# Six more of the late tiles' products joined into sevens of quarter products, and the left-hand sums of three joins moved to GpSimd

## Chip, cores and metric

One NeuronCore of a Trainium2 chip. The metric is the device time of one launch in microseconds (us). Before the change it is 378.43 us, the median of three runs (378.24 to 379.07).

## What is computed

Attention with softmax over 8 batches, 12 heads, 448 tokens and head width 64, followed by a feed-forward layer with a SiLU-gated hidden layer on the same 3584 tokens. Cut to what matters:

```python
scores = scale * np.matmul(q, k.transpose(0, 1, 3, 2))
attn = np.exp(scores - max); attn = attn / sum
x = np.matmul(attn, v)   # as (3584, 768)
h = x @ w_in             # (3584, 2048)
g = h * (1.0 / (1.0 + np.exp(-h)))
return g @ w_out         # (3584, 768), float32
```

The change touches the last product alone, g @ w_out, for the rows that are computed last.

## The kernel before, in words

The rows of the output are cut into 28 tiles of 128 tokens, and two neighbouring tiles make a **quad** (qd 0 to 13). For a quad, the product with w_out is a 2 by 2 block product: two row tiles against the two halves of the hidden dimension, and these against the two halves (384 columns each, `OH`) of w_out. The kernel does it with **seven block products instead of eight** (Winograd's form of Strassen's scheme). The products are numbered m = 1 to 7; each is eight matmuls (`HF` = 8 hidden tiles of 128) of 128x384. Their left operands are blocks of the hidden values `G` (and `X`, a copy of one tile of `G`) or sums of such blocks (`S`, written by DVE in `combine_g`, two instructions of 128x512 for each sum; product 7's sum is written over `G`). Their right operands are blocks of w_out or differences of them (`D4`, `D5`, `D6`). PSUM results are copied to `ost` tiles by ACT (`take_copy`, products 1, 5, 6, 4) or added to them by DVE (`take_sum`, products 2, 7, 3), and stored by DMAs from SP and ACT.

A **fold** goes one level deeper. The same product m of two quads a and b has the same right operand; so the two left operands, of two different quads, stand above each other and make another 2 by 2 block product, with the eight hidden tiles cut 4 and 4 and the 384 columns cut 192 and 192. A fold does it with seven products of four matmuls of 128x192 (`fold_product`, k = 1, 4, 6, 5, 7, 3, 2 in two PSUM banks `n_..._P` and `n_..._Q`) instead of 16 matmuls of 128x384. It needs four sums of left blocks (`fold_x`, 128x512 f16, by DVE, L1065) and, once for each m, four differences of right blocks (`fold_w`, 128x768, by DVE, L1047). `fold_read` adds the results into the output tiles (DVE, L1101 to L1113), or copies the first of them where the fold is listed in `AHEAD_OF` (ACT, L1097). Before, `FOLD` (L254) names three folds: m = 2 and m = 4 of quads 10 and 11, and m = 4 of quads 12 and 13.

**The order of all work is laid out ahead of time** by a planner in the kernel (`Order`, L111, `step`, L160): it keeps a clock for each engine, gives each operation a planned cost, and appends the instructions to the engines' queues in the order in which it thinks that they become ready. TensorE (PE) takes from the list `moe` the first entry whose inputs are ready in the planner's time. On the chip, every engine then goes through its queue strictly in that order and waits on semaphores. The costs in the planner are its author's numbers (0.40 for an instruction of `combine_g`, 0.43 for one of `fold_x`, for instance); they only set the order.

The end of the kernel is in this order: the hidden values of the last two pairs of batches (products `f`, L683 through `times`, read by ACT and DVE), then quads 10 to 13. GpSimd (POOL) issues the loads of q, k, v and the weights and has nothing to do after the last of them.

Rings limit how far engines may run ahead: `S` has three buffers (`NSG`), `ost` four (`NOST`); some quads' output tiles lie in old buffers instead (`FAR` in the `xT` ring, `WIDE` in two `E` slots).

Of the kernel before, what the change touches and what calls it, by code (L numbers as in the profile page):

```python
# [110 lines left out]
class Order:  # L111


    def __init__(self, shy):
        self.now, self.shy = 0.0, shy
        self.free = {"PE": 1.0, "ACT": 2.1, "DVE": 1.2, "POOL": 1.2}
        self.wait = {"ACT": [], "DVE": []}
        self.pool = []
        self.sent = []
        self.dma_free = 0.0  # L120
        self.out = []
        self.mode = None
        self.drawn, self.crossed = 0, [0.0]
        self.busy = {e: 0.0 for e in self.free}
# [35 lines left out]
    def step(self):  # L160

        soon = []
        for eng in ("ACT", "DVE"):
            if self.free[eng] > self.now:
                soon.append(self.free[eng])
                continue
            best, urgent = None, None
            for op in self.wait[eng]:
                at = op.ready()
                if at is None:  # L170
                    continue
                if at > self.now:
                    soon.append(at)
                    if op.bias <= -10 and (urgent is None or at < urgent):
                        urgent = at
                elif best is None or (rank(op), at + op.bias) < best[0]:
                    best = ((rank(op), at + op.bias), op)
            if best and best[1].bias >= 0 and eng == "DVE" and urgent is not None:
                if urgent < self.now + self.shy * best[1].busy:
                    continue  # L180
            if best:
                self.wait[eng].remove(best[1])
                self.start(best[1])
                soon.append(self.free[eng])
        if self.free["POOL"] > self.now:
            soon.append(self.free["POOL"])
        elif self.pool:
            op, took, ring, gate = self.pool[0]
            at = 0.0
            if ring is not None:  # L190
                at = ring.when(1)
            if at is not None and len(self.sent) >= LOADS:
                at = max(at, self.sent[-LOADS].done + HOP)
            if at is not None and gate is not None:
                g = gate()
                at = None if g is None else max(at, g)
            if at is not None and at <= self.now:
                self.pool.pop(0)
                if ring is not None:
                    ring.take()  # L200
                self.start(op)
                self.sent.append(op)
                took += DMA_SLOW if len(self.sent) == 3 else 0.0
                few = len(self.sent) < 7
                start = self.now + DMA_START + (0.0 if few else DMA_LATE)
                self.dma_free = max(self.dma_free, start) + took
                op.done = self.dma_free + DMA_TAIL + (0.0 if few else DMA_MORE)
                soon.append(self.free["POOL"])
            elif at is not None:
                soon.append(at)  # L210
        return soon
# [3 lines left out]
def kernel(  # L215
# [36 lines left out]
    FAR = (NT * B // 4 - 3, NT * B // 4 - 1)  # L252
    WIDE = (NT * B // 4 - 6, NT * B // 4 - 4)
    FOLD = ((10, 11, (2, 4)), (12, 13, (4,)))  # L254
    AHEAD_OF = ((1, 4),)
# [649 lines left out]
    def combine_g(qd, m, f0, f1):  # L905
        a, b = 2 * qd, 2 * qd + 1
        if m != 7 and (qd, m) not in S_t:
            S_t[(qd, m)] = sb.tile([128, HF, 128], FP16, name=f"S_{qd}_{m}", tag="S", bufs=NSG)
# [12 lines left out]

    def product(qd, m, f0, f1, strips, c0=0, c1=OH):
        w = {1: rows(2 * qd, 0), 2: rows(2 * qd, 1), 4: rows(2 * qd + 1, 1), 7: rows(2 * qd + 1, 0)}
        w = w[m] if m in w else S_t[(qd, m)]
        if BANK[m] == m and f0 == 0:
            pr_t[(qd, m)] = psum_bank(f"p_{qd}_{m}" + "r" * (c0 > 0))
        if c1 - c0 < OH:
            half_t[c0] = pr_t[(qd, m)]
        for f in range(f0, f1):
            times(  # L930
                pr_t[(qd, BANK[m])][:, 0 : c1 - c0],
                w[:, f, :],
                W_[m][:, f, c0:c1],
                f == 0 and BANK[m] == m,
                f == HF - 1,
                strips,
            )
# [24 lines left out]
    def ost(qd, i, j):  # L962
# [4 lines left out]
        elif qd in WIDE:  # L967
            at, x = int(i != j), j
            if (qd, at) not in wide_t:
                wide_t[(qd, at)] = sb.tile(  # L970
                    [128, HG, S], FP16, name=f"wide_{qd}_{at}",
                    tag=f"E{e_slot[f'sx_{PAIRS[0]}_{at + 1}']}", bufs=1,
# [42 lines left out]

    def take_last(qd):
# [12 lines left out]
    def left(q, m, k):  # L1029
        return rows(2 * q + m // 4, 1)[:, 4 * k : 4 * k + 4]  # L1030
# [3 lines left out]

    def right_sum(m, i):
        n = 4 * (m // 4) + i - 1
        t = w_in_t[:, n % NDC, DFF // 2 * (n // NDC) : DFF // 2 * (n // NDC) + 2 * OH]
        return t.rearrange("p (f n) -> p f n", f=4)
# [10 lines left out]
    def fold_x(g, m, i, at):  # L1049
# [3 lines left out]
        if tag == "KT":  # L1053
# [11 lines left out]
        nc.vector.tensor_tensor(out=x2_t[(g, m, i)], in0=x, in1=y, op=op)  # L1065

    def fold_product(g, m, k):
# [12 lines left out]
        if k in (1, 4):  # L1080
            t = ps.tile([128, 2, 512], FP32, name=f"n_{g}_{m}_{bank}", tag="s", bufs=2)
            n2_t[(g, m, bank)] = t[:, 0, :]
# [4 lines left out]
    def fold_read(g, m, k):  # L1087
        a, b = FOLD[g][:2]
        i, j = {2: SUM[2], 4: OUT[4]}[m]
# [163 lines left out]
    far_ring, wide_ring = Ring(NX3), Ring(0)  # L1253
# [170 lines left out]
    def queue_pair_f(pb, f):  # L1424
# [23 lines left out]
        def queue(m):  # L1448
# [6 lines left out]
            def run():  # L1455
# [8 lines left out]
                if pb == PAIRS[0] and f == (3 if FILL < 4 else HF - 1) and m == 4:  # L1464
                    last_pair.append(op)
                    for _ in range(4):
                        wide_ring.give(op.done)
                if m == 1:
# [17 lines left out]
            def deps():  # L1486
# [14 lines left out]
                if before is not None:  # L1501
                    made.append((before.get(m), 9.0))
                if m == 1:
# [80 lines left out]
    def plan_sums():  # L1584
# [12 lines left out]
        while todo and (todo[0] == 7 or sg_ring.can(1, od.now)):  # L1597
            m = todo.pop(0)
            if m != 7:
# [23 lines left out]
    def plan_folds():  # L1623

        last = PAIRS[1]
        if "w" not in w2_op and (last, 5) in pair_done:
            made = [pair_done[(last, f)].get(m) for f in range(6) for m in range(1, 8)]
            if None not in made:
                w2_op["w"] = True
                for m in sorted({m for *_, ms in FOLD for m in ms}):  # L1630
                    for i in (1, 2, 3, 4):
                        more = [w2_op[(m, i // 2)]] if i in (2, 4) else []
                        w2_op[(m, i)] = od.add(
                            Op("DVE", 0.57, lambda m=m, i=i: fold_w(m, i), made + more, 1)
                        )
        if not folds or (last, HF - 1) not in pair_done:
            return
        g, m, done = folds[0]
        made = [x for q in FOLD[g][:2] for f in range(HF, NFF) for x in gates_at(2 * q + m // 4, f)]
        made += [pair_done[(last, HF - 1)].get((i, j)) for i in range(2) for j in range(2)]  # L1640
        n = len(x2_op) // 4
        if n > 1:
            made += [fold_done[n - 2].get(k) for k in (7, 2)]
        if None in made:
            return
        folds.pop(0)
        homes = [("KT", 3)] * 3 + [("rk", NRK)] if n % 2 else [("rq", NRQ)] * 4
        for i in (1, 2, 3, 4):
            more = [x2_op[(g, m, i // 2)]] if i in (2, 4) else []
            x2_op[(g, m, i)] = od.add(  # L1650
                Op("DVE", 0.43, lambda i=i: fold_x(g, m, i, homes[i - 1]), made + more, 1)
# [5 lines left out]
    def queue_fold(g, m):  # L1657
# [4 lines left out]
        first = {2: 1, 4: 4}[m]  # L1662
        early = (g, m) in AHEAD_OF
        if early:
            ahead[a] = lambda: when([reads.get(2)])
            ahead[b] = lambda: when([reads.get(7)])
        home = {q: far_ring if q in FAR else wide_ring if q in WIDE else ost_ring for q in (a, b)}

# [5 lines left out]
        def queue(k):  # L1674
            rings = ((s_ring, 1),) if k in (1, 4) else ()
# [3 lines left out]
            def run():  # L1679
                op = Op("PE", 4 * mm(OH // 2), lambda: fold_product(g, m, k), tail=PE_OUT)  # L1680
                for ring, need in rings:
                    ring.take(need)
                od.on_pe(op, "full", 4)
                done[k] = op
                narrow, wide = OH / 1920.0 + 0.13, OH / 960.0 + 0.13
# [6 lines left out]
                elif k == 7:  # L1692

                    def then(at):
                        s_ring.give(at)
# [8 lines left out]
                elif k == 2:  # L1704

                    def then(at):
                        s_ring.give(at)
# [5 lines left out]
            def deps():  # L1713
                made = [done.get(x) for x in {6: (1,), 5: (4,), 7: (6, 5), 3: (5,), 2: (3,)}.get(k, ())]
                made += [reads.get(x) for x in {6: (1,), 7: (6,), 3: (5,)}.get(k, ())]
                if not early:
                    made += [took_of[a].get(first)] if k == 1 else [took_of[b].get(first)] if k == 4 else []
                if (g, m) == TAIL and k in (2, 3):
# [8 lines left out]
                if not i:  # L1727
# [4 lines left out]
            moe.append((deps, 0, run, rings))  # L1732
# [6 lines left out]
    def queue_quad(qd):  # L1739
        quads.append((qd, [5, 6, 7, 3]))  # L1740
        took = {}
        home = far_ring if qd in FAR else wide_ring if qd in WIDE else ost_ring
# [13 lines left out]
        def queue(m, f0, f1, c0=0, c1=OH):  # L1756
            first = {6: (1,), 2: (1,), 7: (6, 5), 3: (5, 6) if qd == LAST else (5, 6, 7), 4: (7,)}.get(m, ())

            def run():
# [7 lines left out]
                if BANK[m] == m and f0 == 0:  # L1767
                    take_bank(f"p_{qd}_{m}" + "r" * (c0 > 0))
# [14 lines left out]
                read(m, [op] + [took[x] for x in {2: (1,), 7: (5,), 3: (6,)}.get(m, ())])  # L1783
                if m == 7 and (qd, 4) in folded:
                    if qd in ahead:
                        def then(at):
# [8 lines left out]
                                [op, took[7], ahead[qd]],  # L1795
# [7 lines left out]
            def deps():  # L1803
# [4 lines left out]
                made += [took.get(x) if x in hard else (took.get(x), 9.0) for x in first]  # L1808
# [8 lines left out]

            rings = ((home, 1),) if f0 == 0 and (m in OUT or m == 7 and (qd, 4) in folded and qd not in ahead) else ()
            moe.append((deps, int(BANK[m] == m and f0 == 0), run, rings))


# [6 lines left out]
        for m in (1, 5, 6, 2, 7, 3, 4) if qd < LAST else (1, 5, 6, 7, 3, 4):  # L1828
            if m == (3 if TAIL and qd == LAST else 4):
                for g, (a, b, ms) in enumerate(FOLD):  # L1830
                    for k in ms if max(a, b) == qd else ():
                        if (g, k) not in AHEAD_OF:
                            queue_fold(g, k)
# [449 lines left out]
```

## Time and profile before

| | us |
|---|---|
| median of three runs | 378.43 |
| the profiled execution | 378.51 |
| its span, first to last instruction | 376.7 |
| PE busy | 370.6 |
| DVE busy | 284.5 |
| ACT busy | 255.6 |
| POOL busy | 85.0 |

The span lies 1.8 us inside the profiled execution's time. "Busy" counts the time in which at least one instruction of the engine runs; a PE that is always busy may still be waiting for the next matmul's turn in its pipeline, and the time from one matmul's start to the next says more than the length of one. A group line gives line, engine, operation, output and inputs, count, busy us and mean ns. A window line gives for each engine its busy us and, in brackets, its instructions.

### The profile page before, as it was taken

The page shows a single profiled execution, that of the slowest core. Times are in us where ns is not written, and L with a number is a line of the kernel's source. Part 1 is how long each engine was busy: PE and PEld are TensorE (multiplying, and loading weights), DVE is VectorE, ACT ScalarE, POOL GpSimd, SP SyncE. Part 2 cuts the span into 40 slices and gives each one's busy share as a digit, 9 for nine tenths or more (in the row PEclk, how much of TensorE's full clock was granted, in tenths as well). Part 3 has the DMA queues.
Part 4 walks back from the last instruction along what each step waited for, and adds up shares of the span by engine and source line. Part 5 has one row for each costly group of instructions (what it writes and reads, how often), then busy time and mean ns, then how long its engine had stood idle before and what let it go on. Part 6 is the DMA issues. An engine that isn't in the chain of part 4 may idle for free.

```text
span 376.7 us, 9950 instructions
## 1 busy us (share of the span) xinstructions
PE 370.6 (98%) x4018; PEld 187.2 (50%) x4018; DVE 284.5 (76%) x588; ACT 255.6 (68%) x401; POOL 85.0 (23%) x155
## 2 busy tenths in 40 slices
PE   7999999999999999999999999999999999999996
PEld 3365445444444444444444454545556655556764
DVE  3668859899995969995969998899375425489953
ACT  4988873896878787877788777658872238883130
POOL 6652438324016326006423200000000000000000
PEclk9999999999999999999999999999999999999999
DMA  7999999919049848147955411210002330001334
GB/s 121 185 208 210 206 204 198 189 19 132 17 96 153 153 50 124 27 99 107 170 91 72 55 44 44 54 33 0 0 3 56 88 92 19 0 0 29 83 104 125
DMA packets 35967, 34.47 MB, mean 91 GB/s; under 512 B 11857, under 2 KB 35153, under 8 KB 35921
## 3 DMA queue, kind: packets, MB, share of 16 engines
q0 software_dynamic: 25312, 22.82, 40.8%
q1 hardware_dynamic: 10064, 10.38, 10.2%
q8 instruction: 31, 0.51, 0.6%
q10 hardware_dynamic: 544, 0.64, 0.5%
q14 instruction: 16, 0.12, 0.1%
HBM read 45.61 MB, written 11.01 MB: 150 GB/s over the span
## 4 chain that ended last, share of the span: by engine, by line
PE 95%; DVE 1%; ACT 1%; DMA 1%; issue 0%; DVEq 0%; POOLq 0%
PE p L683 30%; PE h L683 21%; PE f L683 16%; PE s L446 11%; PE a L568 8%; PE o L683 3%; PE a L554 2%; PE a L601 2%; PE n_Q L683 1%; DMA rk<-in_k_dram 1%; ACT T L491 1%; PE n_P L683 1%; PE z L683 0%; PE z L2185 0%; PE z L554 0%
## 5 line engine op out<-in xcount | busy, mean ns | idle before, releaser
L502 ACT ACTIVATE E<-s 128x896 f16<-128x896 f32 x164 | 141.9, 923 | 24.5 <-PE s L446 24.5
L683 PE MATMUL h<-xT,w_in_t 128*32 128x448 f16 (+2 forms) x762 | 83.5, 348 | 0.0
L683 PEld LDWEIGHTS <-w_in_t 128*128 128x128 f16 (+1 forms) x909 | 54.6, 97 | 50.0 <-issue 8.1
L352 POOL DMA_DIRECT2D V<-in_v_dram x88 | 48.5, 560 | 50.7 <-PE a L568 29.3
L683 PEld LDWEIGHTS <-G 128*128 128x128 f16 (+1 forms) x672 | 42.4, 97 | 29.5 <-issue 5.0
L715 ACT ACTIVATE th<-h 128x448 f16<-128x448 f32 x67 | 36.6, 546 | 24.2 <-PE h L683 21.0
L683 PE MATMUL p<-w_out_t,G 128*128 128x384 f16 (+2 forms) x326 | 50.6, 324 | 0.0
L446 PE MATMUL s<-rq,KT 32*128 32x448 f16 (+3 forms) x728 | 45.0, 347 | 1.5 <-DVE rq L410 1.0
L683 PEld LDWEIGHTS <-S 128*128 128x128 f16 (+1 forms) x321 | 29.5, 98 | 22.3 <-issue 3.4
L1004 ACT COPY ost<-p 128x384 f32<-128x384 f32 x42 | 20.1, 479 | 29.2 <-PE p L683 22.8
L759 DVE SCALAR_TENSOR_TENSOR G<-th,h 128x448 f16<-128x448 f16 (+1 forms) x64 | 35.6, 572 | 4.7 <-ACT th L715 4.3
L683 PE MATMUL p<-D,S 128*128 128x384 f16 (+1 forms) x217 | 38.8, 326 | 0.0
L1023 DVE TENSOR_TENSOR ost<-p,ost 128x384 f32<-128x384 f32 x31 | 17.1, 552 | 22.2 <-ACT ost L1004 14.5
L568 PE MATMUL a<-E,V 128*32 128x448 f16 (+1 forms) x640 | 32.7, 356 | 0.0
L332 POOL DMA_DIRECT2D rq<-in_q_dram x25 | 14.0, 559 | 68.1 <-PE s L446 59.0
L671 DVE SCALAR_TENSOR_TENSOR xT<-a,rdn 128x448 f16<-128x448 f32 x46 | 26.9, 618 | 2.9 <-PE a L568 2.2
L446 PEld LDWEIGHTS <-KT 32*128 32x128 f16 (+1 forms) x824 | 12.4, 96 | 31.7 <-issue 29.5
L515 DVE TENSOR_TENSOR T<-T,E 128x1792 f16<-128x1792 f16 x21 | 22.8, 1085 | 4.8 <-ACT E L502 4.8
L515 DVE TENSOR_TENSOR T<-E,E 128x1792 f16<-128x1792 f16 x21 | 22.7, 1082 | 4.0 <-ACT E L502 4.0
L886 DVE TENSOR_TENSOR p<-f,p 128x448 f32<-128x448 f32 x15 | 9.3, 623 | 19.2 <-PE f L683 11.5
L683 PE MATMUL f<-sx,tw 128*128 128x448 f16 x102 | 23.4, 352 | 0.0
L568 PEld LDWEIGHTS <-V 128*32 128x32 f16 (+1 forms) x640 | 13.5, 95 | 18.1 <-issue 10.1
(128 smaller groups left out, 455.1 us busy)
## 6 DMA issues: line engine op xcount, KB each, us to landing
out_dram<-ost SPq DMA_DIRECT2D x163, 48.0 KB, 1.7
rk<-in_k_dram POOLq DMA_DIRECT2D x24, 224.0 KB, 5.2
rq<-in_q_dram POOLq DMA_DIRECT2D x23, 224.0 KB, 5.8
w_out_t<-in_moe_w_out_dram POOLq DMA_DIRECT2D x4, 768.0 KB, 12.9
V<-in_v_dram POOLq DMA_DIRECT2D x42, 64.0 KB, 4.3
V<-in_v_dram POOLq DMA_DIRECT2D x42, 48.0 KB, 4.6
w_in_t<-in_moe_w_in_dram POOLq DMA_DIRECT2D x6, 256.0 KB, 8.7
w_in_t<-in_moe_w_in_dram POOLq DMA_DIRECT2D x3, 512.0 KB, 12.5
```

What stands on the lines that cost most here:

```text
L332: nc.gpsimd.dma_start(out=rawq[n][:, cols], in_=group_of(q, b, hg)[:, cols])
L352: nc.gpsimd.dma_start(out=VT[b][32 * x : 32 * (x + 1), hs, at : at + count, :], in_=v[b, hs].rearrange("h (i g) d -> i h g d", g=TPP)[:, : ...
L446: nc.tensor.matmul(out=pS[p0 : p0 + 32 * (x1 - x0), h % 2, at : at + q1 - q0], lhsT=KT[(b, hg)][32 * h : 32 * (h + 1), key_rows(b, hg, c, ...
L502: nc.scalar.activation(out=E[(n, w)][:, 2 * y : 2 * y + 2, :], in_=pS_t[(n, w, y)][:, :, 0:S], func=AF.Exp, scale=attn_scale,)
L515: nc.vector.tensor_tensor(out=T[n], in0=T[n] if step else E[(n, 0)], in1=E[(n, step + 1)], op=ALU.add,)
L568: nc.tensor.matmul(out=a[32 * h : 32 * (h + 1), 0:S], lhsT=VT[b][k0:k1, HG * hg + h, place(b, hg, c), part - 1 :: 2], rhs=e[k0:k1, h], sta ...
L671: nc.vector.scalar_tensor_tensor(out=x3(b, cc)[:, cc % 3, 32 * g0 : 32 * g1], in0=acc[(n, part)][:, 0:nq], scalar=0.5, in1=rdn_t[n].rearra ...
L683: nc.tensor.matmul(out=out[i : i + cut], lhsT=w[:, i : i + cut], rhs=x, start=start, stop=stop, skip_group_check=True,)
L715: nc.scalar.activation(out=th, in_=h_t[(b, f, t0)][:, 0:n], func=AF.Tanh)
L759: nc.vector.scalar_tensor_tensor(out=dst[:, f, at + lo : at + hi], in0=th_t[(b, f, t0)][:, lo - t0 : hi - t0], scalar=1.0, in1=h_t[(b, f, ...
L1004: nc.scalar.copy(out=ost(qd, *OUT[m]), in_=bank(qd, BANK[m]))
L1023: nc.vector.tensor_tensor(out=t, in0=bank(qd, BANK[m]), in1=t, op=ALU.add)
```

## The change

- `FOLD` now names six folds: also m = 5 of quads 10 and 11, m = 5 of quads 12 and 13, and m = 4 of quads 7 and 8. Six products of the quads (5 of 10, 11, 12, 13; 4 of 7 and 8) thus go from eight matmuls of 128x384 each to their share of seven times four of 128x192.
- The left operands of the folds with m = 5 are the sums `S_..._5`, which now lie in four old buffers of their own. Product 5's result belongs to two output tiles; a new DVE instruction, `take_mix`, adds the one output tile to the other (f32, 128x384, both in SBUF), once for each of quads 10 to 13.
- The four `fold_x` sums of the three folds (0, 2), (0, 4) and (1, 4), that is of m = 2 and m = 4 of quads 10 and 11 and m = 4 of quads 12 and 13, are written **by GpSimd** instead of DVE: 12 instructions of 128x512 f16 with two SBUF inputs. The build puts an instruction that reloads GpSimd's library ahead of the first.
- The differences of right operands for m = 2 and m = 4 are made earlier (beside quads 7 to 9) and into other buffers; four new ones for m = 5 take their place beside the last pair.
- Quad 11's output tiles lie in `E` slots (`BROAD`) instead of `xT` tiles; the fold of quads 7 and 8 uses PSUM banks of the ring `m` instead of `s`; the order in which the planner lays out the last 100 us is another one.

```diff
-    FAR = (NT * B // 4 - 3, NT * B // 4 - 1)
+    FAR = (NT * B // 4 - 1,)
+    BROAD = NT * B // 4 - 3
-    FOLD = ((10, 11, (2, 4)), (12, 13, (4,)))
-    AHEAD_OF = ((1, 4),)
+    FOLD = ((10, 11, (5, 2, 4)), (12, 13, (5, 4)), (7, 8, (4,)))
+    MID = 2
+    AHEAD_OF = ((0, 5), (1, 5), (1, 4))
...
+    def take_mix(qd):
+        t = ost_t[(qd, *OUT[6])]
+        nc.vector.tensor_tensor(out=t, in0=t, in1=ost_t[(qd, *OUT[5])], op=ALU.add)
...
     def left(q, m, k):
-        return rows(2 * q + m // 4, 1)[:, 4 * k : 4 * k + 4]
+        x = S_t[(q, 5)] if m == 5 else rows(2 * q + m // 4, 1)
+        return x[:, 4 * k : 4 * k + 4]
...
-        nc.vector.tensor_tensor(out=x2_t[(g, m, i)], in0=x, in1=y, op=op)
+        eng = nc.gpsimd if (g, m) in ((0,2),(0,4),(1,4)) else nc.vector
+        eng.tensor_tensor(out=x2_t[(g, m, i)], in0=x, in1=y, op=op)
...
             x2_op[(g, m, i)] = od.add(
-                Op("DVE", 0.43, lambda i=i: fold_x(g, m, i, homes[i - 1]), made + more, 1)
+                Op(
+                    *(("POOL", 1.3) if (g, m) in ((0,2),(0,4),(1,4)) else ("DVE", 0.43)),
+                    lambda i=i: fold_x(g, m, i, homes[i - 1]),
+                    made + more,
+                    1,
+                )
             )
```

## Prediction

> **What bounds the kernel now.** I read the page first: busy time, the slices, the chain that ended last. Then the last 40 us in windows, the timeline there, and the groups of DVE and POOL.
>
> ```profile
> PE 370.6 (98%) x4018; PEld 187.2 (50%) x4018; DVE 284.5 (76%) x588; ACT 255.6 (68%) x401; POOL 85.0 (23%) x155
> ...
> POOL 6652438324016326006423200000000000000000
> PEclk9999999999999999999999999999999999999999
> ...
> PE 95%; DVE 1%; ACT 1%; DMA 1%; issue 0%; DVEq 0%; POOLq 0%
> ```
>
> PE holds 95% of the chain at full clock; what shortens PE's list shortens the run, unless PE must wait. POOL is idle from the 24th slice (about 226 us) on. The windows of the last stretch (us, busy of PE, PEld, DVE, ACT, POOL):
>
> ```profile
> 330.00:340.00 10.00, 10.00 (x58) 5.50 (x57) 8.53 (x18) 7.82 (x17) 0.00 (x0) 1.00 0.00 0
> 340.00:350.00 10.00, 10.00 (x70) 6.41 (x68) 10.00 (x30) 2.87 (x6) 0.00 (x0) 1.00 0.16 42
> 350.00:360.00 10.00, 10.00 (x93) 7.99 (x92) 7.93 (x21) 2.55 (x6) 0.00 (x0) 1.00 0.30 75
> 360.00:370.00 10.00, 10.00 (x67) 6.28 (x66) 5.46 (x13) 1.91 (x4) 0.00 (x0) 1.00 0.33 95
> ```
>
> PE has no gap here, and DVE is full from 340 to 350: 10.00 of 10.00. In that window DVE writes the sums that PE multiplies next, so this is the second bound. ACT and the DMAs have room.
>
> **PE's part.** The timeline of PE (start, length; a row's length reaches past the next row's start because matmuls overlap):
>
> ```profile
> 343.12 1.46 PE L683 MATMUL p<-w_out_t,G 128*128 128x384 f16 x8
> 344.42 0.65 PE L683 MATMUL p<-D,S 128*128 128x384 f16 x3
> ...
> 348.49 0.49 PE L683 MATMUL n_P<-w_in_t,fold 128*128 128x192 f16 x4
> 348.82 0.49 PE L683 MATMUL n_Q<-w_in_t,fold 128*128 128x192 f16 x4
> ```
>
> Eight matmuls of 128x384 take 344.42 - 343.12 = 1.30 us, four of 128x192 take 0.33. A fold replaces two products, 2.60 us, by seven fours, 2.31 us. It saves 0.29; three more folds save **0.87 us**.
>
> What PE newly waits for: in the order after the change, the last hidden-layer product is followed by eight matmuls of p_11_1 (1.30), one four of n_0_5_P (0.33), and then n_0_5_Q, which needs both halves of S_10_5 and S_11_5 at once; before, only S_10_5 was needed so early. The four DVE instructions can begin when ACT's last writes of G allow, about 338.5 to 338.65 (the first was at 338.49), follow each other by 0.33, and the last takes 0.42: 340.1, as PE arrives. I allow 0.1 us there and 0.1 for two or three small waits later: 0.2. Without other effects the execution goes from 378.51 to 378.51 - 0.87 + 0.2 = **377.84**.
>
> **What lies beside other work.** DVE, from 338 on: four fewer fold_x (-4 x 0.33; twelve go to GpSimd, eight for m = 5 come), four take_mix and four more fold_read of about 0.55 each (no row has take_mix; the nearest, ost<-n_Q,ost of the same shape, takes 550 ns), or 0.47 when they follow each other: -1.3 + 3.8 = +2.5 us. DVE is idle for 2.07 us in 350 to 360 and 4.54 in 360 to 370, where the take_mix stand, so it costs nothing if the sums keep their places; uncovered, it costs up to 2.5. The eight fold_w of m = 2 and 4 (0.55 each) and four fold_x for quads 7 and 8 move to 280 to 295, where DVE is busy 4.59 of 6 (282 to 288) and 2.79 of 6 (288 to 294): nothing. ACT swaps four copies for six fold reads, of 10 us a window it uses 2.9: nothing. The stores keep their number (203 on SP); some of quads 7, 10 and 11 change places in SP's queue, and with a DMA share of 0.16 to 0.33 they hold up nobody. The end (last product, take_end, its store) is as it was.
>
> **GpSimd's sums.** No row shows GpSimd adding tiles. Its MEMSET of 64x256 takes 330 ns, one of 128x1 about 106: 0.88 ns for an element, 0.45 us for a pass over 512. From below: as fast as DVE's fold_x, 0.41. From above: two reads and a write one after the other, 0.11 + 3 x 0.45 = 1.45. I take two passes, 1.0 us. Their place has room: the first four need only G, can start at 338.5, and PE reads the first of them (fold_0_2_2, third in GpSimd's queue) after 47 matmuls of 384 and eight or nine fours, about 10.5 us after 339.8. The tightest is fold_1_4_2, third of the last four: inputs free at 357, read at 364. Each may take 2.3 us before PE waits. The library reload stands behind GpSimd's last load with no wait, 110 us before its first use: nothing.
>
> [...]
>
> **The step that decides: DVE and GpSimd side by side.** All 12 GpSimd sums read two SBUF tiles, in three bursts of four; beside them DVE runs sums with two SBUF inputs. In the order after, DVE has 26 of these in a row from 338.65. No row shows both engines reading. The nearest:
>
> ```profile
> L916 DVE TENSOR_TENSOR S<-G x26: 404/417/427, 93.3 to 358.5; 128x512 f16<-128x512 f16 x26
> ```
>
> From 93 to 226 us GpSimd issued loads beside these sums, later it did nothing, and minimum and maximum differ by 23 ns: issuing loads does not hurt DVE. But that is not reading tiles. So the ends are: no effect, 0; and taking turns, each DVE sum waiting for a GpSimd sum to finish. DVE has nothing to give in the first burst: 26 x 25 ns = 0.65 us, a lengthening by 6%, already eats the gain. Behind a DVE sum that is held stand all later sums and the reads that free PE's banks. I therefore take **turns**, with this price. Burst one: the four DVE sums that PE waits for stand behind four GpSimd sums, 4 x 1.0, less 0.3 for what PE has in hand: 3.7. Burst two (fold_0_4, about 346 to 351): DVE's run of two-input sums ends soon, then come reads from PSUM; one GpSimd sum counts: 0.8. Burst three (357 to 362): beside S_13_3 and the fold_1_5 sums, which PE needs within 3 us: half of 4, less some slack: 1.5. Together 6.0: 377.84 + 6.0 = **383.8 us**. With 0.55 for a sum (one pass, 0.11 + 0.45) it is 3.3 and 381.1; with 1.45, 8.7 and 386.5. If DVE's run goes first and GpSimd waits for its end at 347.5, the first fold sums come at 350.5 or later and the later ones push on: about half, 381. The case's own range is 380 to 386.8.
>
> [...]
>
> **The rivals.**
>
> 1. *Side by side without harm* (faster or no change). Place: the DVE sums beside a GpSimd sum. Price: none, so 377.84, between 377.6 (all waits gone, 378.51 - 0.87) and 378.2. For it: the row of S<-G. Against: these are loads. It decides as soon as a DVE sum beside a GpSimd sum is lengthened by less than 25 ns. Chance 0.30. The bound of 0.2%, about what a measurement of this kernel can tell from no change, is 0.76 us; 377.84 lies 0.59 under the median of 378.43, so 0.17 of this counts as the same and 0.13 as faster.
> 2. *Some sharing*: DVE sums beside GpSimd's become 50 to 150 ns longer, without turns. About 30 of them: 1.5 to 4.5 us, of which the idle time from 350 on takes half: 378.6 to 380. Chance 0.08, slower.
> 3. *The fold sums come late without any sharing*: GpSimd needs over 2.3 us for each, or its first instruction after the reload over 8 us. At 3 us, the last four end 2.8 us later than allowed, and the two bursts before them 1 to 3: 380 to 385. For it: nothing shows GpSimd's adds. Against: it would be double my upper end. Chance 0.05, slower. It is also the case in which the change does not do what it says: the joined products are there (36 more matmuls), but the relief of DVE isn't.
> 4. *Turns*: for it, DVE's lack of room; against, no row. Chance 0.57, slower.
>
> **How the numbers follow.** The likeliest is turns, 383.8. Slower 0.57 + 0.08 + 0.05 = 0.70; same 0.17; faster 0.13. The range takes in the first rival and the turns up to 386.8: 377.6 to 386.8. These are sums against the profiled execution, 378.51, which is 0.08 above the median; I leave that difference out.
>
> **What would show it.** PE's count must be 4054 matmuls. Right: DVE's two-input sums from 338.5 on with lengths well over 0.42, or gaps before them while a GpSimd sum runs; PE with gaps of some us at about 340, before n_0_5_Q. Wrong: PE without gaps over 0.2 us, DVE sums still at 0.42, and a span near 376.0. GpSimd's row gives the price of its sum (0.41 to 1.45). If the gaps stand before products that read fold_0_2, fold_0_4 or fold_1_4, it is the third rival, or DVE went first. If PE waits in 280 to 300, the moved fold_w were not free, which I have at nothing.

## The result, and the profile after

The kernel after takes **389.66 us**, the median of six runs from 387.18 to 391.00; the kernel before, on the same chip, 378.52. The ratio is 1.0285, 95% interval 1.0266 to 1.0304. The forecast was 383.8, with a range of 377.6 to 386.8: the sign is right, the time lies outside the range. The profiled execution after is 390.25, its span 388.5.

The same lines of the page as were shown of before: busy times, slices of POOL and of PE's clock, the chain.

```profile
PE 376.0 (97%) x4054; PEld 191.6 (49%) x4054; DVE 299.1 (77%) x605; ACT 255.9 (66%) x403; POOL 99.8 (26%) x167
...
POOL 6653448251036233036322100000000000045400
PEclk9999999999999999999999999999999999969989
...
PE 91%; DVE 5%; ACT 1%; DMA 1%; issue 1%; DVEq 0%; POOLq 0%
```

The 36 more matmuls are there (4054). Two things are new: DVE holds 5% of the chain, and the clock's row is no longer all nines: 6 in the 36th slice, 8 in the 39th. The windows of the last stretch (us; busy of PE, PEld, DVE, ACT, POOL; then PE's granted clock):

```profile
330.00:340.00 10.00, 10.00 (x56) 5.36 (x55) 6.86 (x12) 8.00 (x17) 1.01 (x1) 1.00 0.00 1
340.00:350.00 10.00, 6.53 (x27) 3.28 (x25) 10.00 (x21) 1.28 (x3) 3.94 (x4) 0.68 0.01 2
350.00:360.00 10.00, 10.00 (x79) 7.13 (x78) 7.38 (x16) 2.24 (x5) 4.89 (x4) 0.98 0.08 21
360.00:370.00 10.00, 8.03 (x71) 5.96 (x68) 10.00 (x22) 1.28 (x3) 5.00 (x4) 1.00 0.38 99
370.00:380.00 10.00, 9.83 (x74) 7.58 (x75) 5.38 (x11) 2.68 (x7) 0.00 (x0) 0.83 0.21 61
```

Between 340 and 350 PE is busy 6.53 us, DVE is full and has finished 21 instructions where it had 30 before. The timeline there (start, length, engine; in brackets the idle time before and who ended it):

```profile
338.99 1.15 POOL L1103 TENSOR_TENSOR fold<-G 128x512 f16<-128x512 f16 x1 [123.83 <-ACT G L898]
339.12 5.18 DVE L926 TENSOR_TENSOR S<-G 128x512 f16<-128x512 f16 x4 [0.82 <-PE f L687]
...
340.11 1.32 POOL L1103 TENSOR_TENSOR fold<-X,G 128x512 f16<-128x512 f16 x1
...
341.40 1.32 POOL L1103 TENSOR_TENSOR fold<-fold,X 128x512 f16<-128x512 f16 x1
342.80 1.21 POOL L1103 TENSOR_TENSOR fold<-X,fold 128x512 f16<-128x512 f16 x1
...
344.35 0.82 PE L687 MATMUL n_Q<-w_in_t,S 128*128 128x192 f16 x4 [3.37 <-DVE S L926]
```

Four sums of DVE, which follow each other by 0.33 us when nothing holds them, need 5.18 together, nearly as long as the four GpSimd sums beside them (5.02): each lets one of the other engine's go first and ends 0.28 us after it. PE stands 3.4 us for the last of them. The groups of DVE from 338 to 388 say the same by kind: sums with two SBUF inputs that fall beside GpSimd's are stretched (the four of the first burst to 1.31 to 1.37 us, from 0.41), reads with one input in PSUM are not (128x384 in 0.54 to 0.56, beside GpSimd's sums and elsewhere).

```profile
L926 DVE TENSOR_TENSOR S<-G 128x512 f16<-128x512 f16 x8 | 6.7, 883 | 0.8 <-PE f L687 0.8
...
L1040 DVE TENSOR_TENSOR wide<-p,wide 128x384 f32<-128x384 f32 x4 | 2.2, 547 | 0.1
```

What I had not priced is the clock. Its changes lie 6.83, 20.48 and 3.41 us apart here, multiples of 3.41, and these windows are cut on that grid (busy of PE, granted clock):

```profile
336.71:340.12 3.41, 3.41 (x22) 1.00 0.01 2
340.12:343.54 3.42, 0.76 (x6) 1.00 0.02 5
343.54:346.95 3.41, 2.60 (x11) 0.50 0.00 0
346.95:350.37 3.42, 3.42 (x12) 0.50 0.00 0
367.43:370.85 3.42, 1.63 (x16) 1.00 0.41 107
370.85:374.26 3.41, 3.41 (x19) 0.50 0.37 98
```

After the window with 0.76 us of work PE gets **half the clock** for two windows, after the one with 1.63 us for one. So the time has these parts. Waits and slow matmuls are read from the start of one matmul to the next, against the usual 162.6 ns (384 columns) and 82.4 (192); the rest are times of the two profiled executions:

| before to after | us |
|---|---|
| work saved by three more folds | -0.87 |
| PE waits: 3.80 at 340 to 344, 0.66 at 360 to 362, 2.11 at 367 to 370, small ones 0.16; less 0.06 before | +6.67 |
| matmuls at half clock: 6.83 + 3.41 us of it | +4.52 |
| the first hidden-layer product starts later (25.31 to 25.75) | +0.46 |
| from the end of the last product to the end of the span (3.59 to 4.51) | +0.92 |
| sum (the executions differ by 11.74) | +11.70 |

The fourth line isn't the change's: that start lies between 24.87 and 26.41 over all profiles here, before and after alike. The single runs differ mainly by the clock: 387.18 us at a mean clock of 0.995, 391.0 at 0.985. So the 4.52 us are those of the profiled execution (0.986); the faster runs lose less.

### The profile page after: what moved, and what is told of

The parts are those of the page before. It is cut to its first block, busy times and chain, and to the rows that moved or that the text cites. A ratio compares the mean times of both kernels' runs of the same rounds, so it can differ in the third digit from the quotient of the medians.

```text
span 388.5 us, 10054 instructions
## 1 busy us (share of the span) xinstructions
PE 376.0 (97%) x4054; PEld 191.6 (49%) x4054; DVE 299.1 (77%) x605; ACT 255.9 (66%) x403; POOL 99.8 (26%) x167
## 4 chain that ended last, share of the span: by engine, by line
PE 91%; DVE 5%; ACT 1%; DMA 1%; issue 1%; DVEq 0%; POOLq 0%
PE p L687 26%; PE h L687 20%; PE f L687 15%; PE s L450 11%; PE a L572 8%; PE o L687 3%; PE a L558 2%; DVE S L926 2%; PE a L605 2%; PE n_Q L687 1%; PE n_P L687 1%; DMA rk<-in_k_dram 1%; ACT T L495 1%; DVE fold L1103 1%; DVE wide L1031 1%
## 5 line engine op out<-in xcount | busy, mean ns | idle before, releaser
L687 PE MATMUL p<-w_out_t,G 128*128 128x384 f16 (+2 forms) x326 | 53.3, 328 | 0.0
L1103 POOL TENSOR_TENSOR fold<-G 128x512 f16<-128x512 f16 x5 | 5.9, 1197 | 139.6 <-ACT G L898 123.8
L687 PE MATMUL p<-D,S 128*128 128x384 f16 (+1 forms) x185 | 35.6, 343 | 0.0
L1017 ACT COPY ost<-p 128x384 f32<-128x384 f32 x36 | 17.3, 480 | 18.3 <-PE p L687 12.3
L1040 DVE TENSOR_TENSOR ost<-p,ost 128x384 f32<-128x384 f32 x29 | 16.0, 552 | 16.0 <-ACT ost L1017 7.7
```

Source lines behind the costliest of these rows:

```text
L687: nc.tensor.matmul(out=out[i : i + cut], lhsT=w[:, i : i + cut], rhs=x, start=start, stop=stop, skip_group_check=True,)
L1017: nc.scalar.copy(out=ost(qd, *OUT[m]), in_=bank(qd, BANK[m]))
L1040: nc.vector.tensor_tensor(out=t, in0=bank(qd, BANK[m]), in1=t, op=ALU.add)
```

## The experiments

Each is compared with the kernel before on the same chip (378.5 to 378.9). "Tail" is the time from the end of the last product to the end of the span. The first expectations were written with GpSimd's turns and the clock as the theory, and with rivals in which the loss stays when GpSimd's sums are gone.

**e1: all left sums by DVE.** The planner knows it, so the order at the end is another one: the fold (1, 4) ends 2.0 us before the last product, 5.7 in the kernel after, 12.0 in the kernel before.

```diff
-        eng = nc.gpsimd if (g, m) in ((0,2),(0,4),(1,4)) else nc.vector
+        eng = nc.vector
-    *(("POOL", 1.3) if (g, m) in ((0,2),(0,4),(1,4)) else ("DVE", 0.43)),
+    "DVE", 0.43,
```

> The joined products as in the change, but all fold_x sums by DVE (the planner lays out its order anew, with 0.43 for each). Theory A (DVE's and GpSimd's two-input sums take turns, and PE's clock falls when it waits): without GpSimd's sums no DVE sum is held, PE has waits of 0.2 us together and its clock stays at 1.0; 0.87 us less matmul time and 0.2 us of waits give 377.8, between 377.6 and 378.2. Rival B (the extra joined products overload DVE, GpSimd only shows it): DVE has 12 sums of 0.33 us more than in the change, so it is late by up to 4 us and the time is 380 to 390.

380.04 us, ratio 1.0031 (1.0018 to 1.0045). The clock is 1.00 throughout, and one wait is left (0.78). So 9.9 of the 11.1 us went with GpSimd's sums. But it does not reach 377.8: the last product ends at 373.34, 0.20 later than before, and the tail is 5.18. SP's own queue shows the tail; first before, then e1 (the `x` is the number of stores issued in a row):

```profile
364.16 7.84 SPq L997 DMA_DIRECT2D out_dram<-ost  x7
372.94 1.09 SPq L1014 DMA_DIRECT2D out_dram<-ost  x2
```

```profile
355.25 13.56 SPq L1010 DMA_DIRECT2D out_dram<-wide  x27
368.91 5.33 SPq L1010 DMA_DIRECT2D out_dram<-ost  x7
374.33 1.04 SPq L1027 DMA_DIRECT2D out_dram<-ost  x2
```

In e1 SP issues stores without a pause from 355 to 369; a tile that is ready at 362.91 is issued at 366.70. The last two stores, ready at 373.65 and 373.92, go out at 374.33 and 374.89. Neither side of the expectation had that.

**e2: the kernel before, with its twelve sums of `fold_x` on GpSimd.** None of the change's products. The planner knows this too (1.3 for each sum on GpSimd), so some of the work at the end changes places.

```diff
-        nc.vector.tensor_tensor(out=x2_t[(g, m, i)], in0=x, in1=y, op=op)
+        nc.gpsimd.tensor_tensor(out=x2_t[(g, m, i)], in0=x, in1=y, op=op)
```

> The kernel before with its three folds, but the 12 fold_x sums by GpSimd (planned at 1.3): GpSimd's part alone. Theory A: turns as after the change; DVE has no take_mix and less to do, so waits of PE of 5 to 8 us, and a fall of the clock if a wait comes near 3 us, 1.7 to 3.4 us of half speed each: 384 to 391. Rival B (the joined products are the cause): without them the time stays within 1 us of 378.5.

385.40 us, 1.0174 (1.0161 to 1.0187), by the engine of twelve instructions and the order that follows from it. The timeline of DVE has pairs of sums in 2.66 us, and PE waits for them:

```profile
340.63 2.66 DVE L918 TENSOR_TENSOR S<-S,X 128x512 f16<-128x512 f16 x2
343.22 2.66 DVE L918 TENSOR_TENSOR G<-X,G 128x512 f16<-128x512 f16 x2
```

```profile
PE p L685 <- DVE S L918: 3.6, 4, 2.4
```

Waits 5.15, one window at half clock (1.58 us lost), tail 3.60. These are the turns and the fall of the clock, without the change's products and without its order. The expectation had the fall at a wait near 3 us, which no run shows as a limit: the longest wait here is 2.4 us.

**e3, e5, e6: what GpSimd does in place of the sum.** In the place of each of its twelve sums: e3 a sum over 8 columns and two memsets of 128x512 (writes, hardly reads); e5 a sum over half the columns and a memset of the rest; e6 a sum over 8 columns and a copy of 128x512 (one read). The left sums, and with them the output, are then not the reference's; the instructions of the other engines are those of the change.

```diff
 # e3
+        nc.gpsimd.tensor_tensor(out=t[:, 0:1, 0:8], in0=x[:, 0:1, 0:8], in1=y[:, 0:1, 0:8], op=op)
+        for _ in range(2):
+            nc.gpsimd.memset(t, 0.0)
 # e5
+        nc.gpsimd.tensor_tensor(out=t[:, 0:2], in0=x[:, 0:2], in1=y[:, 0:2], op=op)
+        nc.gpsimd.memset(t[:, 2:4], 0.0)
 # e6: the first line of e3, then
+        nc.gpsimd.tensor_copy(out=t, in_=x)
```

> The change with its order on PE, DVE, ACT and SP, but each of the 12 GpSimd sums replaced by a sum over 8 columns (which waits for the same inputs) and two memsets of 128x512; it leaves out 12 sums of the computation. GpSimd is as busy as before (about 1.2 us each) and reads almost nothing. Theory A in the form that reading is what is shared: DVE's sums go back to 0.42, PE's waits to about 0.2 us, clock 1.0: 377.8, up to 378.6 for the small sums. Theory A in the form that any GpSimd instruction holds DVE: as the change, 387 to 391. Rival C (the fold sums reach PE too late): as the change as well, since they are no earlier.

> The change with its order, but each GpSimd sum over half of the hidden tiles (128x256), the other half filled by a memset; it leaves out half of 12 sums. Theory A: a sum holds DVE about 0.6 us instead of 1.2; PE's waits of 6.7 us fall to about 3, the longest from 3.5 to about 1.5, so the clock should not fall (or once, after waits of 2 us in all): 380.5 to 382.5. Rival C (late fold sums): GpSimd's two instructions together take nearly as long as the one sum, so little changes: 387 to 391.

> The change with its order, but each GpSimd sum replaced by a sum over 8 columns and a copy of 128x512 with one SBUF input; it leaves out 12 sums. Theory A, if reading is what is shared: DVE's sums are held for the length of a copy; with 0.6 to 0.8 us for it PE's waits come to 3 to 4.5 us: 380.5 to 384, and more if the clock falls. If only GpSimd's second input mattered, DVE's sums stay at 0.42 and the time is near 377.8.

379.55 (1.0020, 1.0009 to 1.0030), 379.33 (1.0011, 1.0000 to 1.0022) and 379.03 (1.0009, 0.9996 to 1.0022). As whole runs they tell less than planned. The short sums read the first hidden tiles only, so GpSimd's first burst was over before DVE's sums began, and e5 and e6 lie below the times that were expected if reading is shared. e3 lies above its 377.8 to 378.6, by a longer tail. Single instructions tell it. The same DVE sum, first in e6 beside a copy, then in e3 beside a memset:

```profile
358.22 0.61 POOL L1107 COPY fold<-G 128x512 f16<-128x512 f16 x1
358.49 0.62 DVE L1103 TENSOR_TENSOR fold<-S 128x512 f16<-128x512 f16 x1
```

```profile
358.38 1.11 POOL L1108 MEMSET fold<- 128x512 f16 x2
358.39 0.41 DVE L1103 TENSOR_TENSOR fold<-S 128x512 f16<-128x512 f16 x1
```

Beside the copy the sum lasts until 0.28 us after the copy's end; beside the memset it keeps its 0.41. Here it is GpSimd's reading that holds DVE, not its writing. The other direction is in e5: GpSimd comes second, behind a run of DVE sums with no gap.

```profile
345.93 2.06 POOL L1106 TENSOR_TENSOR fold<-G 128x256 f16<-128x256 f16 x1 [8.28 <-DVE fold L1103]
```

A sum that takes 0.66 alone takes 2.06: it ends 0.5 us behind the end of DVE's run (347.47). With GpSimd first, in the kernel after, the engines alternated; here, with DVE first, GpSimd waited for DVE's whole run. PE lost 0.43 us or less in these three, and the clock stayed; yet their tails are 5.26, 4.81 and 4.67.

**e4: the kernel after, with matmuls of zeros at PE's two long waits** (15 and 7, of 512 columns), ahead of the products that wait.

```diff
+        for _ in range({(0, 5): 15, (1, 5): 7}.get((g, m), 0) if k == 4 else 0):
+            nc.tensor.matmul(out=n2_t[(g, m, bank)], lhsT=zeros, rhs=zeros[:, 0:1].to_broadcast([128, 512]), start=True, stop=True)
```

> The change, with matmuls of zeros in PE's two long waits: 15 of 128x512 ahead of n_0_5_Q and 7 ahead of n_1_5_Q, into the bank that the product then starts anew. Theory A: the sums are held as before, PE waits as long, but no longer idles; the clock stays at 1.0 and the 4.5 us of half speed go: 385 to 386 (389.7 less 4.5, plus up to 0.6 where the zeros are longer than the wait). Rival D (the clock falls for another reason, such as the load of all engines): half speed stays, 389 to 391.

385.91 us, 1.0190 (1.0175 to 1.0205): 3.75 less than after, though the sums come as late as there. The first window, which had 0.76 us of work, now has 3.32, and the clock stays:

```profile
340.12:343.54 3.42, 3.32 (x19) 1.00 0.02 5
343.54:346.95 3.41, 3.30 (x22) 1.00 0.00 0
```

The seven zeros do not fill the second wait. They write the bank that the product waits for, so they wait with it (1.61 us, until 367.07) and then run for 1.52 us; the windows around them have 2.86 and 2.52 us of work. They take up the next wait of 0.50, so the edit costs about 1 us of its own, and its gain is net of that. The clock is a term of its own, some 4 us. The tail is 3.87 here, with the same order of the work as after.

**e7: only the fold (1, 4) by GpSimd**, the other eight sums by DVE. The planner lays out the order anew; it is nearly that of e1.

```diff
-        eng = nc.gpsimd if (g, m) in ((0,2),(0,4),(1,4)) else nc.vector
+        eng = nc.gpsimd if (g, m) in ((1,4),) else nc.vector
```

> The change with only the fold of m = 4 of quads 12 and 13 on GpSimd (four sums instead of twelve; the other eight by DVE; the planner lays out its order anew). Theory A: nothing is held before about 357 us, the third burst's turns remain: waits of 2 to 3 us, 0.87 saved, a fall of the clock possible (1.7 us): 379.5 to 382.5. Rival B (joined products overload DVE): DVE has eight sums more than in the change, 385 or more.

382.67 us, 1.0104 (1.0084 to 1.0124), a little over what was expected: four sums cost 2.6 us against e1. Waits 1.59, 0.51 and 1.05, no half clock: the window with the first two still has 1.74 us of work.

**e10: the kernel after, each GpSimd sum cut into two of 128x256.** Result, order and dependences as after.

```diff
-        eng.tensor_tensor(out=x2_t[(g, m, i)], in0=x, in1=y, op=op)
+        for c0, c1 in ((0, 64), (64, 128)) if eng is nc.gpsimd else ((0, 128),):
+            eng.tensor_tensor(out=t[:, :, c0:c1], in0=x[:, :, c0:c1], in1=y[:, :, c0:c1], op=op)
```

> The kernel after with each GpSimd sum written as two instructions of 128x256 (64 of the 128 tokens each); the result and the order are the same, and all of it still needs the last hidden tile. Theory 1 (a DVE sum waits for one GpSimd instruction, so shorter ones hold it less): a turn takes about 0.8 instead of 1.32 us, the four DVE sums that PE waits for end some 2 us earlier, the wait before n_0_5_Q falls from 3.5 to about 1.5, the first stretch at half clock goes, and the time is 383 to 386. Theory 2 (what DVE loses is the sum of GpSimd's reading time, and shorter turns only spread it over more sums): the wait before n_0_5_Q falls, but other waits of the first burst come in its place, 3 to 4 us in all; time 386 to 389. If GpSimd now loses its turn and waits for the end of DVE's run: wait before n_0_5_Q under 0.5, waits before products that read fold_0_2, and a time of 379 to 384.

385.30 us, 1.0176 (1.0163 to 1.0190). It goes as in theory 2 of the expectation: a turn is shorter, and more sums get one. The time is that of theory 1, because the half clock goes.

```profile
338.87 3.24 DVE L926 TENSOR_TENSOR S<-G 128x512 f16<-128x512 f16 x4 [0.82 <-PE f L687]
342.03 1.70 DVE L926 TENSOR_TENSOR S<-S,X 128x512 f16<-128x512 f16 x2
343.65 1.69 DVE L926 TENSOR_TENSOR G<-X,G 128x512 f16<-128x512 f16 x2
```

Eight sums are held now, not four. PE waits 1.87 + 0.47 + 1.29 = 3.63 us in the first burst, 3.80 in the kernel after: cut in two, GpSimd's sums cost PE about as much. The 4.4 us gained are about the clock's 4.52: no window had less than 2.06 us of work, and the clock did not fall. (The tail, 5.39, is 0.88 longer than after; the waits are some 0.8 us less.) That is in part luck with where the 3.41 us windows begin: e13 below has the same sums and the same first waits, but one of its windows held only 1.53 us of work, and half clock followed.

**e8, e9, e11: the tail and SP's queue.** e8 is e1, e9 the kernel before, with the second and fourth store of each tile of quads 10 and 11 issued by GpSimd; e11 is e8 with one more store, `ost_12_10`, there.

```diff
+            if turn % 2 and qd in (10, 11):                                      # e8, e9
+            if turn % 2 and qd in (10, 11) or qd == 12 and (i, j) == OUT[4]:     # e11
+                eng = nc.gpsimd
```

> All left sums by DVE, as in e1, and the second and fourth store of every output tile of quads 10 and 11 is issued by GpSimd, which has nothing else to do then, instead of SP. The order on PE, DVE and ACT is that of e1. Theory (the end is late because SP's stores queue up: in e1 the last product ends at 373.34 and the span 5.18 us later, 3.59 in the kernel before): SP issues 8 stores fewer of about 0.45 us each, so the last ones are issued when their data are ready, the tail falls from 5.2 to 3.6 to 4.0 us, and the time from 380.0 to 378.4 to 378.9. Rival (the tail is long because the stores themselves are slow side by side, whoever issues them): tail stays at about 5, time 379.7 to 380.3.

> The kernel before with the same edit: the second and fourth store of quads 10 and 11 issued by GpSimd. In the kernel before the last stores are issued as soon as their data are ready (0.01 us later), so both theories expect no change: tail 3.5 to 3.7, time within 0.3 us of the kernel before on the same chip. If it gets faster too, e8 tells nothing of the change's own tail.

> e8 with one more store moved from SP to GpSimd: that of ost_12_10 (128x384), which becomes ready with the last products in the order of the change (0.4 us before the last product ends; 8.5 us before it in the kernel before) and stood in SP's queue ahead of the two last stores (issue 0.09, 0.70 and 1.19 us after the last product in e8; -0.20 and 0.42 for the last two in the kernel before). Theory (what is left of the longer end is that three tiles become ready together in the last us and queue behind one another): the last two stores are issued 0.4 to 0.5 us earlier, the tail falls from 4.62 to 4.1 to 4.3, and the time from 379.8 to 379.2 to 379.5. It does not reach the 3.6 of the kernel before, since the last stores' data are ready 0.58 us after the last product, 0.41 there. Rival (the end is long because the transfers of the last us share the engines' bandwidth): the last issues come earlier, the tail stays within 0.15 of 4.62, and the time at 379.6 to 380.

e8: 379.78 us, 1.0030 (1.0020 to 1.0041); e9: 378.67, 1.0006 (0.9996 to 1.0016), no change, tail 3.58. In e8 every late store is issued when ready, except three that become ready together at the end; the tail falls from 5.18 to 4.62, not to 3.6 to 4.0. The theory of the full queue holds for 0.56 us of 1.6. In the profiled executions of e8 and e9 a tile of K, whose load GpSimd issued at the same point as in e1, took 7.1 us to land, 1.7 more, which cost some 0.6 us at 126 us. The edit is not the reason: the same load takes 7.06 in e4 and 6.87 in e5, which have no late store on GpSimd, and 4.4 to 5.4 in all other profiles, e11 and e14 among them. Nor does it keep e8 from 378.4, since e14 below has no such delay and the same time.

e11: 384.15 us, 1.0143 (1.0125 to 1.0161), far from both expectations. After its last store GpSimd stays in a closing DRAIN for 7.78 us, and the span ends with it. Such a DRAIN stands behind GpSimd's last work in every kernel here, for 6.66 us behind the last load in the kernel before and 7.06 behind the last sum in the kernel after, but elsewhere it ends in time (7.65 in e8, until 371.90). The trace still answers the question: the last two stores of SP are issued 0.37 and 0.41 us earlier than in e8, and the last packet lands 3.16 us after the last product, 3.11 in e8. So what is left in e1's order fits the bytes: 0.78 MB are moved after the last product in e8 and e11, 0.44 in the kernel before. That they come so late because the fold (1, 4) ends late is argued from the order, not shown by a run.

**e12, e13, e14: loads of PE's program.** The kernel after, e3, e5, e6 and e10 have another order at the end (the fold (1, 4) ends 5.7 us before the last product), and in e4 that order has a tail of 3.87. What differs is where a packet of the instruction queue falls. In the kernel after, from 380 to 384 (SP's and ACT's stores, then the queue's packets):

```profile
379.93 4.02 ACTq L1010 DMA_DIRECT2D out_dram<-ost  x4
379.94 4.49 SPq L1010 DMA_DIRECT2D out_dram<-ost  x5
```

```profile
q8 instruction: 1, 0.02, 2.7%
```

The packet (16 KB) lies 3.51 us before the last product's end; one store of SP (1.545 us, 0.47 in the kernel before) and one of ACT (1.566, 0.54) are slow behind it, and the last four stores of SP stand behind these. In e3, e5, e6 and e10 the packet lies 3.44 to 3.55 us before that end, with stores of 1.7 to 2.2 us on SP and 1.1 to 1.6 on ACT; in e4, with 44 instructions more, 5.77 before, and no store is slow. From 225 us on such packets lie some 230 to 270 instructions of PE apart, before and after, and the last ones move when PE's instructions are added, so they are taken for loads of its program. It has 8158 instructions after and 8086 before, where the last one lies 15.1 us before the end. All three kernels cut the first zero matmuls into smaller ones, 70 instructions more: e12 in the kernel before, e13 in e10, e14 in e8.

```diff
+        if not spare_seen:
+            wide = 1
+            spare_seen.append(i)
```

> The kernel before; only the first stretch of zero matmuls, at 1.0 to 6.3 us, is cut into 47 matmuls of 128x128 instead of 11 of 128x512 and one of 128x384. PE's program grows by 70 instructions to 8156 (8158 in the kernel after); the same columns stream, and everything from the first load on is as in the kernel before. Theory (a further load of 16 KB of PE's program comes some 250 instructions after the last one and meets the last stores): a packet of the instruction queue shows 2 to 5 us before the last product's end, stores on SP or ACT beside it take 1.1 to 2.2 us instead of 0.35 to 0.54, the tail grows from 3.6 to 4.4 to 5.3, and the time by 0.8 to 1.7 us over the kernel before. Rival (the tail comes from the order of the products and the stores alone): tail 3.5 to 3.7, time within 0.3 us of the kernel before.

> e10 (the kernel after with each GpSimd sum cut in two) with the same 70 instructions more at the start. The loads of PE's program come 70 instructions earlier in the work, the last one some 8 to 9 us before the last product's end instead of 3.45, where no store of quads 12 and 13 is issued. Theory: no store of the last 5 us takes over 0.8 us, the tail falls from 5.39 to 3.6 to 4.0 and the time from 385.3 to 383.5 to 384.2. Rival (order alone): tail 5 to 5.5, time 385 to 385.6.

> e8 (all left sums by DVE, stores of quads 10 and 11 by SP and GpSimd) with the same 70 instructions more at the start; the last load goes from 2.2 to about 7 us before the last product's end. In e8 no store near the end was slow, yet three tiles become ready within the last us, and 0.78 MB are moved after the last product, 0.44 in the kernel before. Theory (there the longer end is the bytes and the order): tail stays at 4.4 to 4.7 and the time at 379.5 to 380.0. Rival (the load was the cause there as well): tail 3.6 to 4.0, time 378.7 to 379.2.

e13: 383.82 us, 1.0137 (1.0112 to 1.0162), against 385.30. The tail falls from 5.39 to 3.59; the packet now lies 5.92 us before the end. Stores of SP and ACT, first in e10, then in e13:

```profile
374.02 4.92 SPq L1010 DMA_DIRECT2D out_dram<-ost  x6
374.45 4.56 ACTq L1010 DMA_DIRECT2D out_dram<-ost  x5
```

```profile
373.79 3.45 SPq L1010 DMA_DIRECT2D out_dram<-ost  x6
374.22 3.68 ACTq L1010 DMA_DIRECT2D out_dram<-ost  x5
```

The same stores take 1.5 and 0.9 us less. e14: 379.91 us, 1.0026 (1.0012 to 1.0040), tail 4.68: in e8's order the load was not the cause, as expected. e12 missed: 379.02, 1.0005 (0.9993 to 1.0017), tail 3.59. A packet did come, 3.82 us before the end, but it slowed one store only (865 ns, 468 in the kernel before), and 0.36 us of pause behind that store took it up. So the late load cost 1.80 us of tail where stores stand close behind one another, in the change's order (e10 against e13); in the order of the kernel before it cost nothing (tail 3.59 in both). None of these kernels beats the kernel before.

## Why the prediction was wrong

- **The bound, the matmuls saved, the small waits: right.** PE's work falls by 0.87 us, the small wait before `n_0_5_P` is 0.27 (I had 0.2 in all for such waits). DVE's full window is where it broke. One reading was off, without effect: GpSimd's last load starts at 214.1 us, not at about 226.
- **"It costs nothing if the sums keep their places": right.** With DVE left alone (e3, e5, e6), PE waits 0.15 to 0.43 us in all. With all sums on DVE (e1) 0.85.
- **GpSimd's sum: 1.0 taken, 1.15 us measured** when it starts alone, 1.21 to 1.32 in its turns in the first burst; between the bounds of 0.41 and 1.45. That the price of the first burst fits all the same is partly luck: a held sum comes every 1.30 us, and since it needs 0.33 anyway, about 1.0 is lost by each, which is what I had taken for the GpSimd sum's own length.
- **The step that decides, turns: right, and close in size.** 3.80 (with that small wait), 0.66 and 2.11 us with the three bursts, where I had 3.7, 0.8 and 1.5: 6.57, against 6.0 and the 0.2. In the second burst what was held longest was a `take_mix` (1.32 us instead of 0.55), which I had counted with the harmless work; PE's wait follows it, at 360.5. e2 shows the mechanism without the rest of the change, e6 and e3 that reading is what counts.
- **The step that failed: the sum itself.** It ran "377.84 + 6.0", as if a wait of PE cost its own length. The clock that PE loses by waiting stood nowhere, neither in the time nor in the bounds that made the upper end of 386.8. It cost 4.52 us, and e4 takes it away. Without it the time lies inside the range (385.91 in e4). I had read `PEclk` all nines in the kernel before and carried it over to a kernel in which I let PE wait 3.7 us in one place.
- **"The end (last product, take_end, its store) is as it was", and the stores "hold up nobody": failed, 0.92 us.** In the kernel after it is the load of PE's program, which 72 more instructions push into the last stores: e13 shows it by the move of the load alone, in e10's kernel, and e4, with the order of after and the load earlier, has a tail of 3.87. In the order of e1 it is SP's full queue (0.56 us, e8) and, as far as e11 and e14 tell, the bytes that become ready late. The forecast of 383.84 with 0.47 more for the waits (6.67 against 6.2), 4.52 for the clock, 0.92 for this and 0.46 for the start gives 390.21; the profiled execution is 390.25.
- **The rivals.** Side by side without harm is refuted by every trace in which a sum on GpSimd starts ahead of DVE's (after, e2, e4, e7, e10, e13). Its price was about right for the case that did not occur: e6, whose GpSimd hardly reads beside DVE's sums, has 379.03 with a tail 1.08 longer than before; without that it would be 377.95, an estimate from these two, where I had 377.84. "Some sharing" falls with the lengths (1.31 to 1.37 us instead of 0.42, not 0.05 to 0.15 more), "late without sharing" with the list of PE's waits, in which all four large ones of the kernel after end with a result of DVE, none with one of POOL.

What stays open: why the K tile lands late in some profiles (e4, e5, e8, e9), and why a packet of the instruction queue makes a store slow.

## What to carry to other kernels

Before giving work to an idle GpSimd, look at what DVE does at that moment: here, while GpSimd read SBUF, DVE's sums of two SBUF tiles followed each other by 1.30 us instead of 0.33, and with GpSimd's sums cut in two PE still waited 3.63 of 3.80 us. When a change makes PE wait, price the wait and the clock after it (6.67 and 4.52 us here): lay the waits on the grid of 3.41 us, and where a window has as little work as those that were followed by half clock here (0.76 to 1.63 us), add up to 1.7 us for the next, an estimate from half of 3.41. Where the grid begins differs from run to run (a window begins at 340.12 us in the kernel after, at 339.19 in e13, at 341.12 in e10), so this gives a range and not one number. And after any change in the number of PE's instructions, look at what the last loads of its program meet (1.80 us of tail between e10 and e13).

## What the runs showed of the hardware

- **Half clock came without a long pause.** Windows of 3.41 us with 0.76, 1.01 (e2), 1.53 (e13) and 1.63 us of PE work were followed by half clock, windows with 1.74 (e7), 2.06 and 2.30 (e10) were not. Busy time alone does not tell it: behind the last product, windows with 1.43 (e14), 1.47 (e1) and 1.56 us of work (e2) were not followed by half clock. In the one with 1.53 the longest single wait was 1.88 us; in the one with 1.63, waits of 2.1 us in all (1.61 and 0.50) were enough.
- **Turns have a grain.** With GpSimd first, in the kernel after, one DVE sum went between two GpSimd sums, and a held sum ended 0.28 us after the GpSimd instruction. With DVE first and without gaps, in e5, GpSimd waited for the whole run (2.06 us for a sum of 0.66).
- **Late work on GpSimd prolonged e11.** A closing DRAIN, counted from its issue, took 7.65 to 7.78 us with its last store in e8, e9, e11 and e14, and 6.35 to 7.21 with its last load, sum, copy or memset in the other kernels (6.66 before, 7.06 after). Only in e11, where the last store goes out 0.15 us after the last product, does the span end with it (7.78 us).
